# Where the first unit's products stand, and which engine scales the weight taps, in a convolution with batch norm and SiLU

## The chip, the cores and the metric

The kernel runs on one core of a Trainium2 chip. A core has five engines with queues of their own: TensorE (PE; its weight loads are listed as PEld), VectorE (DVE), ScalarE (ACT), GpSimd (POOL) and SyncE (SP), which here only issues transfers. The metric is the device time of one execution in microseconds (us); the time of a kernel is the median of its runs. Beside it there is one profiled execution, from which all lines of the profile are.

## The reference

A convolution of three taps along the sequence, with a 1024 x 1024 matrix for each tap, then batch norm with given statistics, then SiLU:

```python
B, S, C = 2, 2048, 1024
K = 3
xp = jnp.pad(x, ((0, 0), (P, P), (0, 0)))
y = sum(jnp.einsum('bsc,cd->bsd', xp[:, k:k + S, :], w[k]) for k in range(K))
inv_std = 1.0 / jnp.sqrt(var + 1e-5)
y = (y - mean) * (g * inv_std) + b
return _silu(y)
```

All inputs and the output are bf16.

## The kernel before

**The method.** Six neighbouring outputs are made at once from eight inputs (a Winograd convolution with six outputs and three taps). The sequence of 2048 falls into 342 such tiles. For each batch the eight combinations of the inputs (matrix `BT`) are made once, and for each the channel product with a combination of the three weight taps. So in place of 3 x 6 products of a tile there are 8, numbered 0 to 7. Products 0 and 7 use the raw taps w[0] and w[2]; products 1 to 6 use sums and differences of scaled taps. The outputs are then combinations of the eight products.

**Batch 0's windows** (L369 to L389 in the listing below: the first loop over `wi`). `x` arrives in 17 windows of 21 tiles (the last of 6) through SP's queue. For each window PE multiplies by the small matrix `Rm` (`transform`, L218; L230 in the profile), eight matmuls in two halves of four, each into a pair of PSUM banks, and ScalarE (L244) or VectorE (L246) casts the half to bf16 into `T_sb0`. Which of the two does it is decided while the kernel is built: `load` holds a planned time for each, and the smaller sum gets the cast. From window 10 on three pairs of banks are used in turn; banks 2 and 3 are then free for products. The raw taps of the first 128 output channels (chunk 0) come between windows 3, 8 and 16, tap w[1] last.

**Batch 1's windows.** The same for `T_sb1`, but in 51 groups of three, three and two matmuls, each into one of banks 4 to 7 in turn. Among them stand the products of the first unit.

**Units.** A unit is one chunk of 128 output channels for one batch: 8 products of 8 matmuls (one for each 128 input channels) with 342 moving columns. There are 8 x 2 units. `mms` (L248; L255 in the profile) is one product. `unit` (L274) yields after every matmul, and `run(gen, n)` takes the next n, which is how the first unit (unit 0) is spread among the transforms. The order of the products is 1, 3, 2, 4, 5, 7, 6, 0, in four banks A, B, C, G: 1 and then 2 into A, 3 and then 4 into B, 5 and then 6 into C, 7 into G. Between two products in one bank ScalarE copies the first one out (`copy_out`, L299; copies m1, m3, m5, s1, s2, L303 in the profile), and VectorE makes the outputs y0 to y5 from banks and copies (`stt`, L295; L296 and L340 in the profile). Product 2 cannot start before m1 is copied, 4 not before m3, 6 not before m5. Unit 0 alone has products 7 and 0 first: columns 0 to 188 (`seven_cut = 9 * WT`) of product 7 one or two matmuls at a time after windows 10 to 15, product 0 over all 342 columns after the last window, and its copy p0; the rest of product 7 stands before product 1 (half of it) and after product 5.

**The `late` list.** The SiLUs of a unit (`silu`, L265; L266 in the profile: y2 and y4 together, then y1, y3 and y5, then y0) are put on the list `late` and issued in the next unit, ahead of its copies; `pace` says how many ahead of which copy (m1, m3, s1, s2, m5 in order of issue); what is left goes after m5. `finish` issues the transposing transfer and the stores of an earlier unit on SP.

**Weight combinations.** For each chunk GpSimd makes three sums of w[0] and w[2] (`pair_sum`, L158: e1, e2, eh) and from each a sum and a difference with w[1] (`pair_tap`, L171), the weights `uch` of products 1 to 6. For this w[0] and w[2] are scaled by 4 and w[1] by 2 (`scale_weights`, L144): on ScalarE (L151), for chunk 0 on GpSimd (L149). From chunk 2 on VectorE makes e1 (`outer_by_reduce`, L165). Chunk 1's work is issued between unit 0 and unit 1 (chunk 0, batch 1): e1 and its two taps, then all three scalings, then the rest.

Every engine works through its own queue in the order in which the kernel text issues; nothing is reordered between engines but by semaphores.

Of the kernel before, what the change touches and what calls it, by code (L numbers as in the profile page):

```python
# [9 lines left out]
ALU = mybir.AluOpType  # L10
# [23 lines left out]
WT = 21  # L34
# [3 lines left out]
def kernel(  # L38
# [14 lines left out]
    CT = C // P  # L53
    DC = D // P
    assert S % P == 0 and C % P == 0 and D % P == 0
    NTB = (S + M_OUT - 1) // M_OUT
    assert NTB <= 512
    NWIN = (NTB + WT - 1) // WT
# [85 lines left out]
    def scale_weights(dc, taps=(2, 1, 0), on_gpsimd=False):  # L144
        for k in taps:
            f = 2.0 if k == 1 else 4.0
            dst = wx[dc, k] = wtmp.tile([P, CT, P], BF16, name=f"w{k}x")
            if on_gpsimd:
                nc.gpsimd.tensor_scalar(dst, raw[dc][k], f, 0.0, op0=ALU.mult, op1=ALU.add)  # L149
            else:  # L150
                nc.scalar.mul(dst, raw[dc][k], f)  # L151
# [24 lines left out]
    load = {"act": 0.0, "dve": 1.0}  # L176
# [68 lines left out]
        else:  # L245
            nc.vector.tensor_copy(dst, src)  # L246

    def mms(bk, j, dc, bi, c0, c1, start, at=0, cts=range(CT)):  # L248

        for ct in cts:  # L250
            if j in (0, 7):
                lhsT = raw[dc][0 if j == 0 else 2][:, ct, :]
            else:
                lhsT = wts[dc][:, j - 1, ct, :]
            nc.tensor.matmul(  # L255
                ps_all[:, bk * 512 + at:bk * 512 + at + c1 - c0],
                lhsT=lhsT,
                rhs=T_sb[bi][:, ct, j, c0:c1],
                start=start and ct == 0,
                stop=ct == CT - 1,  # L260
                skip_group_check=not start,
            )
            yield
# [7 lines left out]
            scale=sk[:, dc:dc + 1],  # L271
        )

    def unit(dc, bi, c0, c1, banks, yT, late, pace=(1, 0, 1, 1, 0), seven_cut=None, calls=None):  # L274

        nn = c1 - c0
        A, B_, C_, G = [ps_all[:, k * 512:k * 512 + nn] for k in banks]
        bA, bB, bC, bG = banks
        pace = list(pace)

        def et(name):
            return epool.tile([P, NTB], FP32, name=name)[:, 0:nn]

        m1, m3, m5, s1, s2, d1 = (et(n) for n in ("m1", "m3", "m5", "s1", "s2", "d1"))
        y_all = epool.tile([P, M_OUT, NTB], FP32, name="y")[:, :, 0:nn]
        y = [y_all[:, i if calls is None else ENDS.index(i)] for i in range(M_OUT)]

        def stt(o, i0, s, i1, op1=ALU.add):  # L295
            nc.vector.scalar_tensor_tensor(out=o, in0=i0, scalar=s, in1=i1, op0=ALU.mult, op1=op1)  # L296
            load["dve"] += 0.00123 * nn

        def copy_out(dst, src):  # L299
            for _ in range(pace.pop(0)):  # L300
                if late:
                    late.pop(0)()
            nc.scalar.copy(dst, src)  # L303
            load["act"] += 0.001 * nn

        if seven_cut:


            p0 = et("s2")
            yield from mms(bG, 7, dc, bi, c0, c0 + seven_cut, True)  # L310
            yield from mms(bC, 0, dc, bi, c0, c1, True)
            copy_out(p0, C_)
            yield from mms(bG, 7, dc, bi, c0 + seven_cut, c1, True, seven_cut, range(CT // 2))
        yield from mms(bA, 1, dc, bi, c0, c1, True)
        copy_out(m1, A)
        yield from mms(bB, 3, dc, bi, c0, c1, True)
        copy_out(m3, B_)
        yield from mms(bA, 2, dc, bi, c0, c1, False)
        copy_out(s1, A)
        stt(d1, m1, 2.0, A, op1=ALU.subtract)  # L320
        yield from mms(bB, 4, dc, bi, c0, c1, False)
        if seven_cut:
            for i in (2, 4, 0):
                stt(y[i], B_, ALPHA * (2.0 ** i), s1)
        else:
            copy_out(s2, B_)
            for i in (2, 4):
                stt(y[i], B_, ALPHA * 2.0 ** i, s1)
        stt(B_, m3, 2.0, B_, op1=ALU.subtract)
        yield from mms(bC, 5, dc, bi, c0, c1, True)  # L330
        copy_out(m5, C_)
        while late:
            late.pop(0)()
        for i in (1, 3, 5):
            stt(y[i], B_, ALPHA * 2.0 ** i, d1)
        if seven_cut:
            yield from mms(bG, 7, dc, bi, c0 + seven_cut, c1, True, seven_cut, range(CT // 2, CT))
        else:
            yield from mms(bG, 7, dc, bi, c0, c1, True)
        nc.vector.tensor_tensor(y[5], G, y[5], op=ALU.add)  # L340
        yield from mms(bC, 6, dc, bi, c0, c1, False)
        for i in (2, 4):
            stt(y[i], C_, BETA * 0.5 ** i, y[i])
        stt(G, m5, 2.0, C_, op1=ALU.subtract)
        if not seven_cut:
            yield from mms(bA, 0, dc, bi, c0, c1, False)
        for i in (1, 3, 5):
            stt(y[i], G, BETA * 0.5 ** i, y[i])
        if seven_cut:
            stt(y[0], C_, BETA, y[0])  # L350
            stt(y[0], p0, 1.0, y[0])
        else:
            stt(y[0], s2, ALPHA, A)
            stt(y[0], C_, BETA, y[0])

        if calls is None:
            late.extend(lambda i=i: silu(dc, yT, y_all, c0, c1, *i, 2) for i in ((2, 5), (1, 6), (0, 1)))
        else:
            late.extend(lambda i=i: silu(dc, yT, y_all, c0, c1, *i) for i in calls)
# [8 lines left out]
    units = [(dc, bi) for dc in range(DC) for bi in range(B)]  # L368
    late = []  # L369
    with tc.tile_pool(name="xwin", bufs=10) as xpool:  # L370
        first = unit(0, 0, 0, NTB, (0, 1, 2, 3), yTs[0], late, seven_cut=9 * WT)
        for wi in range(NWIN):
            window = load_window(xpool, 0, wi)
            if wi in (3, 8, NWIN - 1):
                load_chunk(0, {3: 2, 8: 0, NWIN - 1: 1}[wi])
            for h in range(2):
                bk = (2 * wi + h) % 4 * 2 if wi < 10 else (0, 6, 4)[(2 * wi + h - 20) % 3]
                transform(0, wi, window, 4 * h, 4, bk, 2, 2 if h == 0 and wi in (4, 9) else 0)
            if wi == 0:
                turn_params()  # L380
            if wi == 5:
                open_chunk(0)
                scale_weights(0, (2,), on_gpsimd=True)
            if wi == 8:
                pair_sum(0, 0)
                pair_sum(0, 1)
                scale_weights(0, (0,), on_gpsimd=True)

            run(first, {10: 1, 11: 1, 12: 1, 13: 1, 14: 2, 15: 2}.get(wi, 0))  # L389
        pair_tap(0, 0, ALU.add)  # L390
        scale_weights(0, (1,), on_gpsimd=True)
        for n, op in ((1, ALU.add), (0, ALU.subtract), (1, ALU.subtract)):
            pair_tap(0, n, op)
        pair_sum(0, 2)
        for op in (ALU.add, ALU.subtract):
            pair_tap(0, 2, op)
        make_params()
        load["act"] = load["dve"] = 0.0

        gi, done = 0, 8  # L400
        run(first, done)
        for wi in range(NWIN):
            window = load_window(xpool, 1, wi)
            for ct0, n in ((0, 3), (3, 3), (6, 2)):
                transform(1, wi, window, ct0, n, 4 + gi % 4, 3)
                gi += 1
                want = 8 + 44 * max(gi - 1, 0) // (3 * NWIN - 1)
                run(first, want - done)
                done = want
        for k in (0, 2, 1):  # L410
            load_chunk(1, k)
        load_weights(1)
        run(first)
# [41 lines left out]
    for ui, (dc, bi) in enumerate(units[1:-1], 1):  # L455
        yT = yTs[ui % 2]
        half = 4 * (ui % 2)
        if bi == 0 and dc + 1 < DC:
            outer_by_reduce(dc + 1)
        if bi == 1 and dc + 1 < DC:  # L460
            open_chunk(dc + 1)
            if dc == 0:
                pair_sum(1, 0)
                for op in (ALU.add, ALU.subtract):
                    pair_tap(1, 0, op)
                scale_weights(1)
            else:
                scale_weights(dc + 1)
            for n in range(0 if dc else 1, 3):
                if n:  # L470
                    pair_sum(dc + 1, n)
                for op in (ALU.add, ALU.subtract):
                    pair_tap(dc + 1, n, op)
        calls = ((0, 2), (2, 6)) if ui == len(units) - 2 else None
        run(unit(dc, bi, 0, NTB, (half, half + 1, half + 2, half + 3), yT, late, calls=calls))
        if ui < len(units) - 2:
            late.append(lambda dc=dc, bi=bi, yT=yT: finish(dc, bi, yT))
        if bi == 1 and dc % 2 == 1 and (dc + 3) // 2 < DC // 2:
            load_weights((dc + 3) // 2)
# [150 lines left out]
```

## Time and profile before

| | |
|---|---|
| time of the runs, median (lowest, highest) | 192.47 us (192.31, 192.87), 3 runs |
| the profiled execution: time / span | 192.21 us / 190.3 us |
| mean granted TensorE clock | 0.993 |
| PE, DVE, ACT, POOL busy, us | 179.7, 159.1, 124.9, 147.0 |
| first transform of batch 0 / of batch 1 | 4.16 / 22.11 us |
| last transform of batch 1 | 38.64 us |
| start of the long unbroken stretch of PE | 43.67 us |
| end of that stretch | 174.7 us |

The span runs from the first to the last instruction on the core; the time has 1.9 us more. The profile gives for each engine when it was busy, and for the chain that ended last which engine or transfer set the time at each moment. Matmuls are pipelined: the row of one ends some 0.17 us after the next could start, so prices of matmuls are taken from start to start, and "x8" in a row means eight instructions merged from the first start to the last end.

### The profile page before, as it was taken

What the parts mean: (1) busy time and instruction counts of PE and PEld (TensorE: products, weight loads), DVE (VectorE), ACT (ScalarE), POOL (GpSimd) and SP (SyncE); (2) the same over time, 40 slices, a digit from 0 to 9 for tenths busy, and PEclk for the clock granted to TensorE, in tenths of its full rate; (3) what the DMA queues carried; (4) which work ended last, traced back from release to release, by engine and by line L of the source; (5) the groups of instructions that cost most, each with busy time, mean ns of one, the idle gap of its engine ahead of it and who ended that gap; (6) DMA issues with size and microseconds to landing.
All of it is one profiled execution on the core that took longest, in us unless ns stands there. A gap on an engine that the chain in (4) does not pass through costs nothing.

```text
span 190.3 us, 3950 instructions
## 1 busy us (share of the span) xinstructions
PE 179.7 (94%) x1416; PEld 126.9 (67%) x1416; DVE 159.1 (84%) x343; ACT 124.9 (66%) x207; POOL 147.0 (77%) x88
## 2 busy tenths in 40 slices
PE   7897999999999999999999999999999999999960
PEld 3766788765666666666666666666666666669850
DVE  6577587997999699969996999699879988788981
ACT  3787798998378627763876487548745873625770
POOL 6537699999999996999699969996999699800000
PEclk9999999999999999999999999999999999999997
DMA  5999998940609298979293899874656556566425
GB/s 130 340 350 310 355 367 238 269 109 5 119 5 202 49 208 220 227 169 199 48 190 60 178 250 204 183 166 88 150 99 135 110 129 118 116 126 163 119 65 101
DMA packets 86759, 31.72 MB, mean 167 GB/s; under 512 B 73364, under 2 KB 82580, under 8 KB 86740
## 3 DMA queue, kind: packets, MB, share of 16 engines
q1 hardware_dynamic: 86637, 31.46, 70.2%
q8 instruction: 11, 0.18, 0.4%
q14 instruction: 8, 0.07, 0.1%
q10 hardware_dynamic: 103, 0.02, 0.0%
HBM read 14.82 MB, written 8.39 MB: 122 GB/s over the span
## 4 chain that ended last, share of the span: by engine, by line
PE 82%; ACT 5%; DMA 5%; DVE 3%; SPq 2%; issue 1%; DVEq 0%; ACTq 0%
PE ps_all L255 74%; PE ps_all L230 7%; DMA xw<-in_x_dram 5%; ACT yT L266 2%; ACT T_sb L244 1%; SPq L215 1%; DVE y L516 1%; PE ps_all L494 1%; DVE T_sb L246 1%; ACT w2x L151 1%; SPq L90 1%; ACT w1x L151 0%; DVE d L516 0%; ACT w0x L151 0%; DVE ps_all L516 0%
## 5 line engine op out<-in xcount | busy, mean ns | idle before, releaser
L255 PE MATMUL ps_all<-T_sb,uch 128*128 128x342 bf16 (+2 forms) x816 | 123.2, 299 | 0.6 <-ACT m L303 0.6
L255 PEld LDWEIGHTS <-uch 128*128 128x128 bf16 x816 | 77.0, 97 | 34.0 <-issue 1.0
L266 ACT ACTIVATE yT<-y,beta,sk 128x684 bf16<-128x684 f32 (+5 forms) x46 | 44.1, 960 | 29.2 <-DVE y L296 28.5
L255 PE MATMUL ps_all<-T_sb,wch 128*128 128x342 bf16 (+4 forms) x280 | 44.2, 296 | 0.3 <-DVE T_sb L246 0.3
L296 DVE SCALAR_TENSOR_TENSOR y<-ps_all,y 128x342 f32<-128x342 f32 x90 | 41.8, 508 | 1.3 <-PE ps_all L255 0.3
L173 POOL TENSOR_TENSOR uch<-e,wch 128x1024 bf16<-128x1024 f32 x16 | 33.8, 2133 | 10.7 <-DVE e L169 4.9
L173 POOL TENSOR_TENSOR uch<-e,w1x 128x1024 bf16<-128x1024 f32 x16 | 34.0, 2142 | 0.6
L173 POOL TENSOR_TENSOR uch<-eh,w1x 128x1024 bf16<-128x1024 f32 x16 | 33.8, 2134 | 0.6
L255 PEld LDWEIGHTS <-wch 128*128 128x128 bf16 x280 | 26.4, 97 | 11.4 <-issue 0.3
L303 ACT COPY m<-ps_all 128x342 f32<-128x342 f32 x45 | 19.8, 442 | 19.1 <-PE ps_all L255 18.6
L244 ACT CAST T_sb<-ps_all 128x672 bf16<-128x672 f32 (+5 forms) x50 | 27.7, 610 | 6.6 <-PE ps_all L230 5.8
L230 PE MATMUL ps_all<-Rm,xw 128*128 128x168 bf16 (+1 forms) x272 | 29.2, 238 | 1.5 <-ACT T_sb L244 0.6
L246 DVE CAST T_sb<-ps_all 128x504 bf16<-128x504 f32 (+4 forms) x35 | 23.2, 699 | 6.9 <-PE ps_all L230 6.4
L230 PEld LDWEIGHTS <-xw 128*128 128x128 bf16 (+1 forms) x272 | 22.5, 100 | 7.3 <-issue 3.3
L296 DVE SCALAR_TENSOR_TENSOR y<-ps_all,d 128x342 f32<-128x342 f32 x45 | 20.3, 507 | 0.5
L296 DVE SCALAR_TENSOR_TENSOR y<-ps_all,s 128x342 f32<-128x342 f32 x31 | 14.4, 507 | 3.3 <-ACT s L303 3.3
L163 POOL TENSOR_TENSOR e<-wch,w2x 128x1024 f32<-128x1024 bf16 x8 | 17.0, 2128 | 0.0
L163 POOL TENSOR_TENSOR eh<-w0x,wch 128x1024 f32<-128x1024 bf16 x8 | 17.0, 2127 | 0.0
L296 DVE SCALAR_TENSOR_TENSOR ps_all<-m,ps_all 128x342 f32<-128x342 f32 x30 | 15.3, 509 | 0.0
L296 DVE SCALAR_TENSOR_TENSOR d<-m,ps_all 128x342 f32<-128x342 f32 x15 | 7.6, 507 | 8.9 <-ACT s L303 8.9
L169 DVE TENSOR_REDUCE e<-wch 128x1024 f32<-128x2048 bf16 x6 | 13.7, 2276 | 0.0
L303 ACT COPY s<-ps_all 128x342 f32<-128x342 f32 x30 | 13.1, 438 | 0.1
(68 smaller groups left out, 85.3 us busy)
## 6 DMA issues: line engine op xcount, KB each, us to landing
xw<-in_x_dram SPq DMA_DIRECT2D x30, 256.0 KB
out_dram<-o_sb SPq DMA_DIRECT2D x30, 192.0 KB
wch<-in_w_dram SPq DMA_DIRECT2D x9, 512.0 KB
out_dram<-o_sb SPq DMA_DIRECT2D x15, 120.0 KB
wch<-in_w_dram SPq DMA_DIRECT2D x6, 256.0 KB
xw<-in_x_dram SPq DMA_DIRECT2D x2, 224.0 KB
out_dram<-o_sb SPq DMA_DIRECT2D x15, 7.5 KB
out_dram<-o_sb SPq DMA_DIRECT2D x15, 0.5 KB
```

The costliest lines, as they stand in the source:

```text
L90: nc.sync.dma_start(out=raw[dc][k], in_=w_all[:, k, :, dc * P:(dc + 1) * P])
L151: nc.scalar.mul(dst, raw[dc][k], f)
L163: engine.tensor_tensor(e, a, c, op=ALU.add)
L169: nc.vector.tensor_reduce(e, taps.rearrange("p k ct d -> p ct d k"), axis=mybir.AxisListType.X, op=ALU.add)
L173: nc.gpsimd.tensor_tensor(wts[dc][:, 2 * n + (op == ALU.subtract)], outer[dc, n], odd, op=op)
L230: nc.tensor.matmul(banks[:, at:at + NJ * ntile], lhsT=xw[0:kk, (ct0 + c) * P:(ct0 + c + 1) * P], rhs=Rm[0:kk, :, 0:ntile], start=True, sto ...
L244: nc.scalar.copy(dst, src)
L246: nc.vector.tensor_copy(dst, src)
L255: nc.tensor.matmul(ps_all[:, bk * 512 + at:bk * 512 + at + c1 - c0], lhsT=lhsT, rhs=T_sb[bi][:, ct, j, c0:c1], start=start and ct == 0, st ...
L266: nc.scalar.activation(yT[:, i0:i1:step, c0:c1], y_all[:, i0:i1:step], ACT.Silu, bias=beta[:, dc:dc + 1], scale=sk[:, dc:dc + 1],)
L296: nc.vector.scalar_tensor_tensor(out=o, in0=i0, scalar=s, in1=i1, op0=ALU.mult, op1=op1)
L303: nc.scalar.copy(dst, src)
```

## The change

Seven things are edited:

- `seven_cut` becomes `cut`, 11 windows (231 columns) instead of 9 (189). Product 7 and now also product 0 are made in two parts, columns 0 to 230 and 231 to 341.
- The first parts are issued after windows 13 (2 matmuls), 14 (2), 15 (4) and 16 (8), instead of one or two of product 7 after windows 10 to 15 and product 0 whole after the last window.
- The second part of product 0 (8 matmuls) stands behind the first three groups of batch 1's transforms; products 1, 3, 2, 4 and 5 and half of the second part of product 7 are spread over the other 48 groups. The second part of product 7 stands whole between products 5 and 6.
- Chunk 0: the scaling of w[1] goes from GpSimd to ScalarE; eh is made before the first tap instead of after the fourth.
- Chunk 1: of the three scalings only that of w[2] is issued ahead of unit 1, the other two from the `late` list, w[1] behind the copy m3 and w[0] behind the copy m5, with the sums and taps that need them.
- `pace` of unit 1 is (0, 1, 2, 1, 0) instead of (1, 0, 1, 1, 0).
- The planned cost of a copy on ScalarE is 0.0013 us for each column instead of 0.001.

```diff
@@ mms: the argument cts (a part of the channel tiles) goes @@
-    def mms(bk, j, dc, bi, c0, c1, start, at=0, cts=range(CT)):
-        for ct in cts:
+    def mms(bk, j, dc, bi, c0, c1, start, at=0):
+        for ct in range(CT):
@@ unit @@
-            load["act"] += 0.001 * nn
-        if seven_cut:
+            load["act"] += 0.0013 * nn
+        if cut:
             p0 = et("s2")
-            yield from mms(bG, 7, dc, bi, c0, c0 + seven_cut, True)
-            yield from mms(bC, 0, dc, bi, c0, c1, True)
+            yield from mms(bG, 7, dc, bi, c0, c0 + cut, True)
+            yield from mms(bC, 0, dc, bi, c0, c0 + cut, True)
+            yield from mms(bC, 0, dc, bi, c0 + cut, c1, True, cut)
             copy_out(p0, C_)
-            yield from mms(bG, 7, dc, bi, c0 + seven_cut, c1, True, seven_cut, range(CT // 2))
...
-        if seven_cut:
-            yield from mms(bG, 7, dc, bi, c0 + seven_cut, c1, True, seven_cut, range(CT // 2, CT))
+        if cut:
+            yield from mms(bG, 7, dc, bi, c0 + cut, c1, True, cut)
@@ batch 0's windows @@
-        first = unit(0, 0, 0, NTB, (0, 1, 2, 3), yTs[0], late, seven_cut=9 * WT)
+        first = unit(0, 0, 0, NTB, (0, 1, 2, 3), yTs[0], late, cut=11 * WT)
...
                 scale_weights(0, (0,), on_gpsimd=True)
-
-            run(first, {10: 1, 11: 1, 12: 1, 13: 1, 14: 2, 15: 2}.get(wi, 0))
+                pair_sum(0, 2)
+
+            run(first, {13: 2, 14: 2, 15: 4, 16: 8}.get(wi, 0))
         pair_tap(0, 0, ALU.add)
-        scale_weights(0, (1,), on_gpsimd=True)
-        for n, op in ((1, ALU.add), (0, ALU.subtract), (1, ALU.subtract)):
+        scale_weights(0, (1,))
+        for n, op in ((1, ALU.add), (0, ALU.subtract), (1, ALU.subtract), (2, ALU.add), (2, ALU.subtract)):
             pair_tap(0, n, op)
-        pair_sum(0, 2)
-        for op in (ALU.add, ALU.subtract):
-            pair_tap(0, 2, op)
         make_params()
         load["act"] = load["dve"] = 0.0
-
-        gi, done = 0, 8
-        run(first, done)
+        gi, done = 0, 0
@@ batch 1's windows @@
                 gi += 1
-                want = 8 + 44 * max(gi - 1, 0) // (3 * NWIN - 1)
+                want = 8 * gi // 3 if gi < 4 else 8 + 44 * (gi - 3) // (3 * NWIN - 3)
                 run(first, want - done)
@@ between unit 0 and unit 1 @@
-            if dc == 0:
-                pair_sum(1, 0)
-                for op in (ALU.add, ALU.subtract):
-                    pair_tap(1, 0, op)
-                scale_weights(1)
...
+                def sums(n, *taps):
+                    scale_weights(1, taps)
+                    pair_sum(1, n)
+                    for op in (ALU.add, ALU.subtract):
+                        pair_tap(1, n, op)
+
+                sums(0, 2)
+                late.insert(1, lambda: scale_weights(1, (1,)))
+                late.insert(2, lambda: sums(1))
+                late.append(lambda: sums(2, 0))
         calls = ((0, 2), (2, 6)) if ui == len(units) - 2 else None
-        run(unit(dc, bi, 0, NTB, (half, half + 1, half + 2, half + 3), yT, late, calls=calls))
+        run(unit(dc, bi, 0, NTB, (half, half + 1, half + 2, half + 3), yT, late, (1, 0, 1, 1, 0) if ui > 1 else (0, 1, 2, 1, 0), calls=calls))
```

For chunks 2 to 7 the scalings, sums and taps are issued in the same order as before.

More of the change, by code (lines that the diff above doesn't have):

```diff
@@ L272, in silu, with unit @@
         )
-    def unit(dc, bi, c0, c1, banks, yT, late, pace=(1, 0, 1, 1, 0), seven_cut=None, calls=None):
+    def unit(dc, bi, c0, c1, banks, yT, late, pace=(1, 0, 1, 1, 0), cut=None, calls=None):
         nn = c1 - c0
@@ L335, in unit @@
             stt(y[i], B_, ALPHA * 2.0 ** i, d1)
-        if seven_cut:
-            yield from mms(bG, 7, dc, bi, c0 + seven_cut, c1, True, seven_cut, range(CT // 2, CT))
+        if cut:
+            yield from mms(bG, 7, dc, bi, c0 + cut, c1, True, cut)
         else:
@@ L344, in unit @@
         stt(G, m5, 2.0, C_, op1=ALU.subtract)
-        if not seven_cut:
+        if not cut:
             yield from mms(bA, 0, dc, bi, c0, c1, False)
@@ L348, in unit @@
             stt(y[i], G, BETA * 0.5 ** i, y[i])
-        if seven_cut:
+        if cut:
             stt(y[0], C_, BETA, y[0])
@@ L461 @@
             open_chunk(dc + 1)
-            if dc == 0:
-                pair_sum(1, 0)
-                for op in (ALU.add, ALU.subtract):
-                    pair_tap(1, 0, op)
-                scale_weights(1)
-            else:
[L468 to L473, printed above, removed]
+            if dc:
+                scale_weights(dc + 1)
+                for n in range(3):
+                    if n:
+                        pair_sum(dc + 1, n)
+                    for op in (ALU.add, ALU.subtract):
+                        pair_tap(dc + 1, n, op)
+            else:
+                def sums(n, *taps):
+                    scale_weights(1, taps)
+                    pair_sum(1, n)
+                    for op in (ALU.add, ALU.subtract):
+                        pair_tap(1, n, op)
[3 more added lines that the diff above has]
+                late.append(lambda: sums(2, 0))
         calls = ((0, 2), (2, 6)) if ui == len(units) - 2 else None
-        run(unit(dc, bi, 0, NTB, (half, half + 1, half + 2, half + 3), yT, late, calls=calls))
+        run(unit(dc, bi, 0, NTB, (half, half + 1, half + 2, half + 3), yT, late, (1, 0, 1, 1, 0) if ui > 1 else (0, 1, 2, 1, 0), calls=calls))
         if ui < len(units) - 2:
```

## The prediction, made before the changed kernel had run

> **What bounds the kernel now.** I read the page first (busy shares, the chain that ended last), then the chain in order of time, then the timelines of PE and ScalarE around the two places where the chain leaves PE.
>
> ```profile
> PE 179.7 (94%) x1416; PEld 126.9 (67%) x1416; DVE 159.1 (84%) x343; ACT 124.9 (66%) x207; POOL 147.0 (77%) x88
> PE 82%; ACT 5%; DMA 5%; DVE 3%; SPq 2%; issue 1%; DVEq 0%; ACTq 0%
> ```
>
> PE is busy 94% of the 190.3 us span and carries 82% of the chain. Only where the chain is *not* on PE can a reordering win time. After the input transfers of the first 13.4 us these are the places that matter here:
>
> ```profile
> 20.54 0.37 DVE T_sb L246
> 20.91 0.04 issue
> 20.95 1.32 PE ps_all L255 x8
> ...
> 39.49 1.06 ACT w2x L151
> 40.55 0.94 ACT w1x L151
> 41.49 0.69 ACT w0x L151
> 42.18 0.16 issue
> 42.34 0.94 ACT yT L266
> 43.28 0.34 ACT m L303
> 43.62 0.04 issue
> 43.67 131.03 PE ps_all L255 x912
> ```
>
> Columns: start, length, what. From 43.67 on PE runs 131 us without a break, so everything earlier that delays 43.67 delays the end one for one, and nothing in those 131 us has to be gained. The PE timeline has a second wait just before:
>
> ```profile
> 38.95 0.43 PE L255 MATMUL ps_all<-T_sb,wch 128*128 128x153 bf16 x4
> ...
> 39.64 3.64 PE L255 MATMUL ps_all<-T_sb,uch 128*128 128x342 bf16 x24 [0.26 <-ACT m L303]
> ```
>
> A matmul row ends some 0.17 us after the next could start, so I count waits from start to start.
> (a) Window 16's last transform could be followed at 20.52; product 0 over all 342 columns starts at 20.95, after DVE's cast: 0.43.
> (b) Four matmuls of 0.07 from 38.95 end the queue at 39.23; product 6 starts at 39.64, after the copy m5: 0.41.
> (c) 24 matmuls of 0.145 from 39.64 reach 43.12; product 2 of unit 1 starts at 43.67, after the copy m1, which stood on ScalarE behind three scalings and a silu: 0.55.
> Together 1.39 us.
>
> **The change part by part.** *Products 7 and 0 cut at 231.* Before: 8 matmuls of 189 columns, 8 of 342, 8 of 153. After: 16 of 231 and 16 of 111. Prices from start to start: 189 columns 0.081 (15.28 to 15.36), 153 columns 0.066 (22.69 to 22.75), 342 columns 0.145 (170.20 to 171.36 for 8). The new widths have near neighbours, 229 and 113:
>
> ```profile
> 171.36 3.81 PE L255 MATMUL ps_all<-T_sb,uch 128*128 128x229 bf16 x37
> ...
> 179.13 2.55 PE L255 MATMUL ps_all<-T_sb,uch 128*128 128x113 bf16 x44
> ```
>
> 36 steps in 3.81 less one duration of 0.25 give 0.099; 43 steps in 2.55 less 0.21 give 0.054 (a short wait is in it). Before 8 x 0.081 + 8 x 0.145 + 8 x 0.066 = 2.34; after 16 x 0.099 + 16 x 0.054 = 2.45: **+0.11**. Bounds for 111 columns: 0.050 to 0.066 (the 153 row), so +0.05 to +0.30.
>
> *Where they stand.* The products after windows 13 and 14 fall into waits that stay (PE stops after 17.96 until 18.38 for a DVE cast). The four after window 15 cost 0.40 instead of 0.16, less 0.09 of wait: window 16 comes 0.15 later and ends at 20.67. Then 8 matmuls of product 0's first 231 columns, which need windows 0 to 10 alone, run to 21.46 while window 16 is cast. So (a) goes, and batch 1's transforms start at 21.46 instead of 22.11. SP's queue keeps its order; its wait for the first part of batch 1's window 0 ends at 21.07, so that data is there. The tails (8 of product 0 behind the first three groups, 4 of product 7 at the end of the loop) are in the +0.11.
>
> *Tap scaling w1x of chunk 0, POOL to ScalarE.* 1.04 on POOL (L149), 1.05 on ScalarE (L151; 0.95 start to start). It stands behind window 16's cast (ends 21.20) and ahead of all casts of batch 1. What hides it is this gap:
>
> ```profile
> 22.53 0.96 ACT L244 CAST T_sb<-ps_all 128x504 bf16<-128x504 f32 x2 [1.33 <-PE ps_all L230]
> ```
>
> Scaling 21.2 to 22.2; group 0's cast, which could start 0.42 after its matmuls (22.11 to 22.53 before), so at 21.88, starts at 22.15 and ends at 22.75. Its bank is wanted by group 4 at 21.46 + 11 x 0.0725 + 8 x 0.054 = 22.69: a wait of 0.1, as long as the one that PE had at the same place (22.97 + 0.07 to 23.19). **0**. Cover gone: up to 0.95.
> The Trainium skill (TensorE: Matmul & The Clock Gate, on engine queue depths) says that ScalarE's queue is a strict FIFO; by this rule a scaling whose tap has not landed would hold all casts behind it. The rows agree with the order (the copy m1 at 43.19 stands behind work that it does not need), and with a landing after 21.2 the sum would lose what it is late by. The landing that POOL waited for ended at 20.41, so I add nothing.
>
> *POOL.* eh (2.13) moves into POOL's idle 2.31 us before 20.41, and w1x leaves. The first tap still runs 20.41 to 22.54; product 1 first reads it at about 23.0. Later taps come up to 3.2 us sooner, and nothing waited for them: **0**. If the first tap were later than 23.0, PE would wait.
>
> *Copy m5.* Product 5 now ends some four groups before the loop does (44 matmuls over 48 groups instead of 50, no product 7 ahead of them), so its copy runs inside the loop: (b) goes. In the loop PE had three short waits near the copies m1, m3 and s1 (0.12, 0.12, 0.19 start to start); a fourth one of that size comes: **+0.14** (bounds 0 and 0.3).
>
> *Chunk 1's scalings apart.* Let T be the issue of batch 1's last transform. PE does 4 tails to T+0.2, product 6 to T+1.4, product 1 to T+2.5. ScalarE does w2x by T+1.3, the copy m1 at T+2.7 to 3.15; product 2 starts at T+3.7: (c) goes. Then silu, copy m3 to T+4.4 (product 4 wants it at T+4.8), w1x, copy s1, silu, copy s2 to T+7.2, copy m5 to T+7.8 (product 6 wants it at T+8.3), silu, w0x to T+9.3. POOL: eh to T+11.4, tap 13.6, tap 15.7; unit 2 starts at T+10.6 and reads them as products 5 and 6 at T+15.2 and T+17.5. Hidden, with at least 1.6 us. But s2 comes 3.4 us ahead of unit 2 instead of 4.0 (46.63 against 50.63), and DVE's outputs behind it 0.6 later against PE. In unit 2 the silu ended at 51.87, copy m1 at 52.49, product 2 at 52.95: 0.6 later just fits; unit 3 may wait a little: **+0.05** (0 to 0.3).
>
> **Sum.** -1.39 + 0.11 + 0.14 + 0.05 = **-1.09**. The profiled execution took 192.21 (span 190.33 and 1.88 around it), 0.26 under the median 192.47 of the three runs. 192.47 - 1.09 = **191.4**.
>
> **Rivals.**
> 1. *ScalarE becomes the loop's bound.*
>
> ```profile
> 22.50:38.90 16.40, 16.38 (x177) 13.43 (x175) 14.18 (x27) 15.21 (x34) 16.16 (x10) 1.00 1.02 299
> ```
>
> (PE, PEld, DVE, ACT, POOL busy.) ScalarE is busy 15.2 of 16.4 us here, and the planner of the casts does not count w1x. If its 0.95 comes back as PE waits: 191.4 + 0.95 = 192.3, no change. Against: the ring of four banks has DVE, with 2.2 us idle, on its other slots, and the gap of 1.33 takes the scaling.
> 2. *Slower: DVE late in unit 1.* The silu ahead of copy m3 needs y2 and y4 of unit 0; I have them at T+2.6. Up to T+3.1 nothing moves, up to T+3.6 PE does not notice; beyond, product 4 waits one for one, and the rest of ScalarE's chain with it. At 2.9 late: 191.4 + 1.9 = 193.3. For: three y operations now stand ahead of the last cast on DVE, and DVE is nearly full in the later units. Against: its 2.2 us idle in the loop.
> 3. *Better.* The short waits near copies vanish, as each group has a little more PE work than before: -1.39 + 0.11 - 0.43 = -1.71, 190.8.
> 4. *The change does not do what it says:* batch 1's first window or tap 1 lands late (the queue is at its full rate there), PE waits at 21.5 and (a)'s share is lost: 192.0.
>
> **How the numbers follow.** A measurement of this kernel can tell about 0.3% (0.58 us) from no change. Forecast 0.62 (own range 190.9 to 191.9), rival 1 0.17, rival 2 0.08, rival 3 0.08, rival 4 0.05. The range 190.7 to 192.3 takes the forecast, rival 4, half of rivals 1 and 3: 0.8. Faster (under 191.9): 0.62 + 0.08 = 0.70; same: rivals 1 and 4, 0.22; slower: 0.08.
>
> **What would show it.** Right: batch 1's first transform near 21.5; w1x on ScalarE between window 16's cast and group 0's; no PE wait at the end of the loop or ahead of unit 1's product 2; the unbroken PE stretch starting 1.1 us sooner. Wrong: PE waits for ScalarE's casts in the loop that sum to over 1 us (rival 1), a PE wait ahead of product 4 in unit 1 or product 2 in units 2 and 3 (rival 2), a PE wait for a transfer near 21.5 (rival 4), or product 1 waiting for POOL's first tap.

## The result: slower by 0.35%, and the profile after

The changed kernel takes 193.25 us (median of 20 runs, 192.74 to 193.90), against 192.59 (20 runs, 192.01 to 193.52) of the kernel before: ratio 1.0035, with an interval of 1.0024 to 1.0047. It was to be 1.09 us faster; it is 0.66 slower.

The page of the changed kernel, the parts with the busy times and with the shares of the chain:

```profile
PE 179.4 (94%) x1424; PEld 126.3 (66%) x1424; DVE 158.7 (83%) x343; ACT 125.7 (66%) x208; POOL 145.8 (76%) x87
...
PE 75%; DVE 9%; DMA 6%; ACT 4%; issue 2%; SPq 1%; DVEq 0%; ACTq 0%
```

Only ScalarE got more work: 125.7 us instead of 124.9, with the scaling w1x of chunk 0. But DVE holds 9% of the chain, where it held 3%, and PE 75% where it held 82%. So somewhere PE now waits for something that goes through VectorE. The chain in order of time (start, length, what) says where:

```profile
33.29 0.51 DVE d L296
33.80 0.61 DVE T_sb L246
...
34.45 0.30 PE ps_all L230 x2
...
39.88 7.34 PE ps_all L255 x53
...
47.29 0.45 ACT m L303
47.74 0.58 ACT yT L266
...
48.34 0.94 DVE y L296 x2
49.27 0.43 DVE ps_all L296
...
53.01 1.79 DVE y L296 x4
```

Two things are new. In the loop the chain leaves PE for `d1` (`d L296`) and a cast. And at 47.21 it leaves PE for the copy m5, a SiLU (`yT L266`) and then VectorE's first `y` of unit 1; there the kernel before had its unbroken stretch of PE. The PE timeline of the changed kernel shows what came of it (the end of a row: what PE waited for):

```profile
40.07 7.13 PE L255 MATMUL ps_all<-T_sb,uch 128*128 128x342 bf16 x48
...
50.52 2.49 PE L255 MATMUL ps_all<-T_sb,uch 128*128 128x342 bf16 x16
53.92 3.64 PE L255 MATMUL ps_all<-T_sb,uch 128*128 128x342 bf16 x24 [0.92 <-ACT m L303]
```

At the end of the loop and ahead of unit 1's product 2 (in the 48 matmuls from 40.07) PE no longer waits: the gains (b) and (c) are there. The new wait is one unit later, ahead of unit 2's product 2 (53.92).

To put numbers on it I take the starts of instructions as milestones. The start of the profiled executions differs for reasons that have nothing to do with the change (batch 0's window 9 begins at 13.43 in the one, 14.02 in the other, after the same transfers and the same work), so stages are counted from window 9 on:

| stage | before | after | difference | predicted |
|---|---|---|---|---|
| window 9 to batch 1's first transform, (a) | 8.68 | 8.15 | -0.53 | -0.65 |
| first to last transform (the loop) | 16.56 | 17.52 | +0.96 | +0.52 |
| to unit 1's product 1, (b) | 2.13 | 1.54 | -0.59 | -0.46 |
| to unit 1's product 2, (c) | 2.87 | 2.32 | -0.55 | -0.55 |
| to unit 2's product 1 | 6.96 | 6.97 | +0.01 | 0 |
| unit 2's product 1 to 2 | 2.32 | 3.40 | +1.08 | +0.05 for this row and the next but one |
| to unit 3's product 1 | 6.97 | 6.96 | -0.01 | 0 |
| unit 3's product 1 to 2 | 2.32 | 2.55 | +0.23 | |
| to the end of the span | 128.09 | 128.08 | -0.01 | 0 |
| sum | 176.90 | 177.49 | **+0.59** | **-1.09** |

In the last column the forecast's +0.11 for the matmuls is spread over the rows in which they stand: -0.22 in (a), +0.38 in the loop, -0.05 in (b).

The sum of +0.59 is close to the 0.66 between the medians, so these stages hold nearly the whole result. Of the 1.68 us between forecast and measurement, 1.26 are in units 2 and 3 and 0.44 in the loop; (a) and (b) differ by 0.12 and 0.13 in opposite directions.

**Units 2 and 3.** VectorE of the changed kernel around unit 1, then ScalarE (start, length, instruction, and in brackets the idle time before it with its releaser):

```profile
48.34 0.94 DVE L296 SCALAR_TENSOR_TENSOR y<-ps_all,s 128x342 f32<-128x342 f32 x2 [2.22 <-ACT yT L266]
```

```profile
46.60 0.44 ACT L303 COPY s<-ps_all 128x342 f32<-128x342 f32 x1
47.29 0.45 ACT L303 COPY m<-ps_all 128x342 f32<-128x342 f32 x1 [0.25 <-PE ps_all L255]
47.63 0.67 ACT L266 ACTIVATE yT<-y,beta,sk 128x342 bf16<-128x342 f32 x1
...
52.58 0.96 ACT L266 ACTIVATE yT<-y,beta,sk 128x684 bf16<-128x684 f32 x1 [3.33 <-DVE y L296]
53.45 0.77 ACT L303 COPY m<-ps_all 128x342 f32<-128x342 f32 x2
```

Unit 1's y2 and y4 (`y<-ps_all,s`) need the copy s2, which ends at 47.04. They start at 48.34, and the releaser is no copy but the SiLU `yT` of 47.63. That SiLU does not make anything they read: it is unit 0's last one, of y0. It *reads* unit 0's `y`. The tile `y` has one buffer, and a new unit opens a new tile in it; the first write to the new tile waits for all reads of the old one, also of slices that this write doesn't touch. Unit 1's new pace (0, 1, 2, 1, 0) leaves this SiLU over until after the copy m5, and m5 waits for product 5 (the 0.25 `<-PE`). From 48.34 on VectorE has one piece of work after the other until unit 1's y2 and y4 are final (52.54); on them wait unit 2's SiLU (3.33 idle) and, behind that in ScalarE's queue, the copy m1, and on this PE.

In the kernel before, the last SiLU stood ahead of s2, the same y operations were released by s2, and unit 2's products 1, 3, 2, 4 and 5 were one row (ScalarE, VectorE and PE of that kernel):

```profile
45.42 0.67 ACT L266 ACTIVATE yT<-y,beta,sk 128x342 bf16<-128x342 f32 x1
46.18 0.45 ACT L303 COPY s<-ps_all 128x342 f32<-128x342 f32 x1
...
46.66 0.94 DVE L296 SCALAR_TENSOR_TENSOR y<-ps_all,s 128x342 f32<-128x342 f32 x2 [0.59 <-ACT s L303]
...
50.63 5.97 PE L255 MATMUL ps_all<-T_sb,uch 128*128 128x342 bf16 x40
```

**The loop.** VectorE and then PE of the changed kernel:

```profile
33.29 0.51 DVE L296 SCALAR_TENSOR_TENSOR d<-m,ps_all 128x342 f32<-128x342 f32 x1 [0.74 <-ACT s L303]
33.72 1.26 DVE L246 CAST T_sb<-ps_all 128x504 bf16<-128x504 f32 x2
```

```profile
33.49 0.31 PE L255 MATMUL ps_all<-T_sb,uch 128*128 128x342 bf16 x1
34.45 0.30 PE L230 MATMUL ps_all<-Rm,xw 128*128 128x168 bf16 x2 [0.65 <-DVE T_sb L246]
```

`d1` needs the copy s1. It stands at the head of VectorE's queue for 0.74 us until s1 comes, and behind it stands a cast, which needs nothing of the kind and whose bank PE wants. PE waits 0.82 from start to start (33.49 + 0.145 to 34.45). The copy s1 is late itself: product 2 ends at 32.06, and s1 starts at 32.81, behind a cast on ScalarE. In the kernel before VectorE had a cast of its own to do ahead of `d1`, and no idle time between the two:

```profile
33.19 0.68 DVE L246 CAST T_sb<-ps_all 128x504 bf16<-128x504 f32 x1 [0.37 <-PE ps_all L230]
33.80 0.51 DVE L296 SCALAR_TENSOR_TENSOR d<-m,ps_all 128x342 f32<-128x342 f32 x1
```

### The profile page after: what moved, and what is told of

Read it like the earlier page. It is cut to its first block, busy times and chain, and to the rows that moved or that the text cites. A ratio compares the mean times of both kernels' runs of the same rounds, so it can differ in the third digit from the quotient of the medians.

```text
span 191.5 us, 3966 instructions
## 1 busy us (share of the span) xinstructions
PE 179.4 (94%) x1424; PEld 126.3 (66%) x1424; DVE 158.7 (83%) x343; ACT 125.7 (66%) x208; POOL 145.8 (76%) x87
## 4 chain that ended last, share of the span: by engine, by line
PE 75%; DVE 9%; DMA 6%; ACT 4%; issue 2%; SPq 1%; DVEq 0%; ACTq 0%
PE ps_all L255 68%; PE ps_all L230 7%; DMA xw<-in_x_dram 6%; DVE y L296 4%; ACT yT L266 2%; ACT T_sb L244 1%; DVE y L519 1%; PE ps_all L497 1%; DVE T_sb L246 1%; DVE ps_all L296 1%; DVE y L340 1%; DVE d L296 1%; ACT m L303 0%; SPq L215 0%; DVE e L169 0%
## 5 line engine op out<-in xcount | busy, mean ns | idle before, releaser
L266 ACT ACTIVATE yT<-y,beta,sk 128x684 bf16<-128x684 f32 (+5 forms) x46 | 44.1, 960 | 30.3 <-DVE y L296 29.6
L296 DVE SCALAR_TENSOR_TENSOR y<-ps_all,y 128x342 f32<-128x342 f32 x90 | 41.9, 508 | 1.6 <-PE ps_all L255 0.6
L244 ACT CAST T_sb<-ps_all 128x672 bf16<-128x672 f32 (+4 forms) x50 | 27.8, 612 | 6.5 <-PE ps_all L230 5.5
L230 PEld LDWEIGHTS <-xw 128*128 128x128 bf16 (+1 forms) x272 | 21.5, 98 | 9.3 <-issue 3.4
L296 DVE SCALAR_TENSOR_TENSOR y<-ps_all,d 128x342 f32<-128x342 f32 x45 | 20.3, 507 | 0.5
L296 DVE SCALAR_TENSOR_TENSOR y<-ps_all,s 128x342 f32<-128x342 f32 x31 | 14.4, 508 | 5.0 <-ACT s L303 2.8
L296 DVE SCALAR_TENSOR_TENSOR ps_all<-m,ps_all 128x342 f32<-128x342 f32 x30 | 15.3, 509 | 0.0
L296 DVE SCALAR_TENSOR_TENSOR d<-m,ps_all 128x342 f32<-128x342 f32 x15 | 7.6, 507 | 9.1 <-ACT s L303 9.1
```

The lines of the kernel that those rows point to most:

```text
L230: nc.tensor.matmul(banks[:, at:at + NJ * ntile], lhsT=xw[0:kk, (ct0 + c) * P:(ct0 + c + 1) * P], rhs=Rm[0:kk, :, 0:ntile], start=True, sto ...
L266: nc.scalar.activation(yT[:, i0:i1:step, c0:c1], y_all[:, i0:i1:step], ACT.Silu, bias=beta[:, dc:dc + 1], scale=sk[:, dc:dc + 1],)
```

## The experiments

Two theories: *turn-over* (the wait in units 2 and 3 comes from the first write to the new `y`, held by unit 0's last SiLU) and *d1* (the loop's loss is `d1` waiting ahead of casts). Against them stand the prediction's first rival (ScalarE has too much work in the loop, by the scaling w1x), its second (y2 and y4 of unit 0 late for the SiLU ahead of m3), and the simpler account that in units 2 and 3 VectorE is late because copies and scalings on ScalarE came later. All ratios are against the kernel before (192.59 us for the changed one, 192.60 in experiments 1 to 4, 192.50 in 5 to 8).

| kernel | median, us | ratio [95%] | loop | wait ahead of unit 2's / 3's product 2 | window 9 to end |
|---|---|---|---|---|---|
| before | | | 16.56 | 0 / 0 | 176.90 |
| changed | 193.25 | 1.0035 [1.0024, 1.0047] | 17.52 | 1.08 / 0.23 | 177.49 |
| 1 one tile y for units 0 and 1 | 192.01 | 0.9956 [0.9938, 0.9974] | 17.53 | 0 / 0.04 | 176.24 |
| 2 last SiLU ahead of s2 | 192.53 | 0.9992 [0.9973, 1.0012] | 17.52 | 0.44 / 0.22 | 176.85 |
| 3 d1 later | 192.43 | 0.9992 [0.9973, 1.0011] | 16.72 | 1.08 / 0.23 | 176.70 |
| 4 w1x back on GpSimd | 193.39 | 1.0037 [1.0023, 1.0052] | 17.58 | 1.08 / 0.22 | 177.61 |
| 5 repairs 1 and 3 | 191.10 | 0.9913 [0.9885, 0.9941] | 16.72 | 0 / 0.05 | 175.44 |
| 6 as 5, old cost of copies | 191.47 | 0.9933 [0.9907, 0.9959] | 16.86 | 0 / 0.05 | 175.57 |
| 7 before + chunk 1's part alone | 193.21 | 1.0034 [1.0014, 1.0054] | 16.56 | 1.08 / 0.23 | 177.65 |
| 8 changed without chunk 1's part | 192.63 | 1.0010 [0.9988, 1.0033] | 17.53 | 0 / 0 | 177.09 |

### 1. Units 0 and 1 share one tile y

```diff
-        y_all = epool.tile([P, M_OUT, NTB], FP32, name="y")[:, :, 0:nn]
+        if (dc, bi) != (0, 1):
+            y_kept[0] = epool.tile([P, M_OUT, NTB], FP32, name="y")
+        y_all = y_kept[0][:, :, 0:nn]
```

Where no new tile is opened, each write waits only for the reads of its own slice.

> The changed kernel, but unit 1 writes its outputs y into the same tile as unit 0 instead of opening a new one in the same buffer; no engine's order changes. Theory (turn-over of y): VectorE's first y operation of unit 1 no longer waits for the last SiLU of unit 0 (which the new pace puts behind copy m5); it starts right behind copy s2, about 1.3 us sooner, PE's waits ahead of product 2 in unit 2 (1.08 us) and unit 3 (0.23 us) shrink to 0.1 us together or less, and the ratio to the kernel before falls from 1.0035 to about 0.997. Rival (VectorE is late from unit 0's own y operations, or from the scaling ahead of copy s1): the first y operation starts at most 0.2 us sooner, both waits stay, ratio about 1.0035.

VectorE, then PE of this kernel:

```profile
46.47 0.94 DVE L298 SCALAR_TENSOR_TENSOR y<-ps_all,s 128x342 f32<-128x342 f32 x2 [0.96 <-ACT s L305]
```

```profile
49.90 5.97 PE L255 MATMUL ps_all<-T_sb,uch 128*128 128x342 bf16 x40
```

The releaser is now the copy s2 (45.99 to 46.44), and unit 2's products 1, 3, 2, 4 and 5 are one row of 40 matmuls without a wait. ScalarE's work and its order are the same as in the changed kernel, the last SiLU still behind m5. So copies and scalings coming later on ScalarE can't be the cause: the turn-over alone cost the 1.24 us between the medians (1.25 in the stages).

### 2. The last SiLU ahead of the copy s2, with a new tile

```diff
-                sums(0, 2)
-                late.insert(1, lambda: scale_weights(1, (1,)))
-                late.insert(2, lambda: sums(1))
+                sums(0, 2, 1)
+                sums(1)
                 late.append(lambda: sums(2, 0))
-        ... (1, 0, 1, 1, 0) if ui > 1 else (0, 1, 2, 1, 0) ...
+        ... (1, 0, 1, 1, 0) if ui > 1 else (0, 1, 1, 1, 0) ...
```

The scaling of w[1] goes back ahead of unit 1, and the SiLU of y0 moves ahead of s2, so that m5 holds nothing.

> The changed kernel, but chunk 1's scaling of w[1] stands ahead of copy m1 (beside that of w[2]) and the three SiLUs of unit 0 all stand ahead of copy s2, as in the kernel before; only the scaling of w[0] stays late. Theory (turn-over of y): as the last SiLU is then done before copy s2, the waits in units 2 and 3 go to 0.1 us or less, unit 1's product 2 still does not wait (ScalarE has 1.3 us idle ahead of copy m1), ratio about 0.997. Rival (VectorE late from unit 0's y operations): the wait ahead of product 2 of unit 2 stays near 1 us, ratio about 1.0035.

Only a part of it came: 0.44 us of the 1.08 stay, and 0.22 in unit 3. VectorE, ScalarE and GpSimd of this kernel:

```profile
44.92 1.98 DVE L296 SCALAR_TENSOR_TENSOR y<-s,y 128x342 f32<-128x342 f32 x1
...
47.98 0.94 DVE L296 SCALAR_TENSOR_TENSOR y<-ps_all,s 128x342 f32<-128x342 f32 x2 [0.65 <-ACT s L303]
```

```profile
46.95 0.67 ACT L266 ACTIVATE yT<-y,beta,sk 128x342 bf16<-128x342 f32 x1 [0.87 <-DVE y L296]
47.52 0.42 ACT L303 COPY s<-ps_all 128x342 f32<-128x342 f32 x1
```

```profile
44.41 4.50 POOL L173 TENSOR_TENSOR uch<-e,w1x 128x1024 bf16<-128x1024 f32 x2
```

VectorE's releaser is the copy s2 again, as meant. But s2 is itself late: it stands behind the SiLU of y0, and that waits 0.87 us for unit 0's last y0 operation, which took 1.98 us here and 0.52 in the changed kernel. The repair ran into another cost, with GpSimd at work beside it (last section).

Four kernels together show how late VectorE may be. Unit 1's first y operation starts so long ahead of unit 2's product 1: before 3.97 us (wait 0), experiment 1 3.43 (0), experiment 2 2.83 (0.44), changed 2.18 (1.08). From 2.83 to 2.18 the wait grows by 0.64 for 0.65; extended back, it begins near 3.3 (an estimate from these two points). The prediction had s2 come 3.4 us ahead of unit 2, and it did (47.04 against 50.52, 3.48): by that alone nothing would have been lost.

### 3. d1 later on VectorE

```diff
-        stt(d1, m1, 2.0, A, op1=ALU.subtract)
+        if cut:
+            load["dve"] += 0.00123 * nn
+        else:
+            stt(d1, m1, 2.0, A, op1=ALU.subtract)
         yield from mms(bB, 4, dc, bi, c0, c1, False)
         if cut:
+            load["dve"] -= 0.00123 * nn
+            stt(d1, m1, 2.0, A, op1=ALU.subtract)
```

In unit 0 d1 is issued after product 4. Its planned load is counted at the old place, so that the planner gives each cast to the same engine as in the changed kernel.

> The changed kernel, but in unit 0 alone VectorE's d1 is issued after product 4 instead of right behind copy s1, so that three casts stand ahead of it; the split of the casts between the engines is the same. Theory (d1 waits in order for copy s1 on ScalarE and holds a cast whose bank PE needs): PE's wait of 0.8 us near 34.4 us goes to 0.2 us or less, the stretch from batch 1's first to its last transform falls from 17.5 us to 16.8 us, ratio about 1.000. Rival (the casts as a whole fill both engines in this stretch, the scaling among them): the wait moves to another group, the stretch stays within 0.2 us of 17.5, ratio about 1.0035.

VectorE of this kernel in the same stretch:

```profile
30.69 2.92 DVE L246 CAST T_sb<-ps_all 128x336 bf16<-128x336 f32 x5
34.00 1.34 DVE L246 CAST T_sb<-ps_all 128x504 bf16<-128x504 f32 x2 [0.39 <-PE ps_all L230]
35.26 0.50 DVE L296 SCALAR_TENSOR_TENSOR d<-m,ps_all 128x342 f32<-128x342 f32 x1
```

VectorE now runs its casts and waits for PE, not PE for it. The loop takes 16.72 instead of 17.52: 0.80 us for moving one operation of 0.51 us, as long as PE's wait of 0.82 had been. The copy s1 starts no sooner (18.80 us after window 9, 18.79 in the changed kernel): its lateness cost PE time only through d1. Units 2 and 3 kept their waits to 0.01 us: the two causes are independent.

### 4. The scaling w1x of chunk 0 back on GpSimd

```diff
-        scale_weights(0, (1,))
+        scale_weights(0, (1,), on_gpsimd=True)
```

> The changed kernel, but chunk 0's scaling of w[1] is back on GpSimd, behind the first tap. Theory (the scaling on ScalarE is hidden in the gap before batch 1's first cast): the stretch from batch 1's first to its last transform stays within 0.2 us of 17.5, ratio 1.0035 within 0.001. Rival 1 of the prediction (the scaling comes back as waits for ScalarE's casts): the stretch shortens by 0.5 to 0.95 us, ratio about 0.9995.

The loop is no shorter (17.58 against 17.52), so ScalarE's added work is not what fills it. ScalarE of the changed kernel shows the cover that the prediction named:

```profile
21.68 1.06 ACT L151 ACTIVATE w1x<-wch 128x1024 bf16<-128x1024 bf16 x1
22.64 1.73 ACT L244 CAST T_sb<-ps_all 128x504 bf16<-128x504 f32 x3
```

The scaling starts when window 16's casts are done, and the first cast of batch 1 follows at 22.64, 0.5 us after its matmuls began.

### 5 and 6. Both repairs; and the old planned cost of a copy

Experiment 5 has the edits of 1 and 3. Experiment 6 has, besides, `load["act"] += 0.001 * nn` as before.

> The changed kernel with both repairs: unit 1 writes y into unit 0's tile, and d1 of unit 0 is issued after product 4. Theory: the two losses are independent, so they add: 193.25 less 1.25 less 0.8 gives 191.2, ratio to the kernel before about 0.9915, no wait of PE above 0.15 us ahead of product 2 in units 2 and 3 nor near 34 us. Rival: they overlap (with the loop shorter, VectorE is later against PE in unit 1 and PE waits in unit 2 again), ratio 0.995 or more.

> As the kernel with both repairs, but the planned cost of a copy on ScalarE is 0.001 us per column again, as in the kernel before, so that some casts go to the other engine. Theory: the cost decides only small waits in the loop (0.3 us in all near 37 us); the time stays within 0.25 us, ratio 0.9915 within 0.0015. Rival: the new cost is what the loop's stretch hangs on; the stretch from batch 1's first to its last transform changes by 0.5 us or more.

Experiment 5 is 0.87% faster than before, the best version, and its chain has no break from unit 0's product 6 on:

```profile
39.54 134.76 PE ps_all L255 x941
```

Counted from window 9 it is 1.46 us shorter than before; the two repairs gained 2.05 together (1.25 and 0.79 alone). With the old planned cost the loop is 0.14 longer; the medians 191.10 and 191.47 lie 0.37 apart, more than the 0.25 expected, but from 6 runs each, and the intervals of their ratios overlap. That the new cost helps here is seen in one profile and not established by the times.

### 7 and 8. The change taken apart

Experiment 7 is the kernel before with chunk 1's scalings apart and the new pace, and nothing else. Experiment 8 is the changed kernel without these two.

> The kernel before with one part of the change alone: chunk 1's scalings taken apart and the pace of unit 1. Theory (turn-over of y): the wait of 0.55 us ahead of product 2 of unit 1 goes, and waits of about 1.1 us ahead of product 2 of unit 2 and 0.2 us in unit 3 come, as VectorE's first y operation of unit 1 now waits for the last SiLU; together 0.75 us more, ratio about 1.004. Rival (the waits in units 2 and 3 come from the earlier start of unit 1 that the cut gives, not from this part): only the gain stays, ratio about 0.997.

> The changed kernel without the part for chunk 1 (its scalings stand together again, pace as before): the cut at 231, the new places, the scaling of chunk 0 on ScalarE and the planned cost remain. Theory: batch 1 starts 0.5 us sooner, the loop is 0.95 us longer (most of it the wait at d1), product 6 does not wait (0.6 us sooner), but product 2 of unit 1 then waits some 0.95 us instead of 0.55 for copy m1 behind three scalings; units 2 and 3 do not wait; together about +0.25 us, ratio 1.001. Rival (the long wait in the loop comes from the part for chunk 1): the loop is as before, ratio 0.996.

PE of experiment 7, then of experiment 8:

```profile
53.79 2.48 PE L255 MATMUL ps_all<-T_sb,uch 128*128 128x342 bf16 x16 [0.92 <-ACT m L303]
```

```profile
44.08 2.19 PE L255 MATMUL ps_all<-T_sb,uch 128*128 128x342 bf16 x14 [0.73 <-ACT m L303]
```

Experiment 7 gains the 0.55 of (c) and loses 1.08 + 0.23, the same as in the changed kernel: chunk 1's part costs by itself, whatever is done in the loop. Its y operation had the same releaser and the same 2.22 us idle before it as the changed kernel's. Experiment 8 has nothing of this, but the wait of 0.55 ahead of unit 1's product 2 has become 0.90 (3.22 between products 1 and 2, against 2.32 without a wait): the loop ends with less for PE to do, product 2 is wanted sooner, and the copy m1 still stands behind three scalings. What (a) and (b) gained goes into this wait and into d1's.

## Why the prediction was wrong

- **(a), (b), (c): right.** The three waits are gone: -0.53, -0.59, -0.55. For (a), batch 1 starts 8.15 us after window 9 (22.17).
- **Products 7 and 0 cut at 231, and w1x: right.** The narrow matmuls need no more than they were given, and experiment 4 shows w1x hidden. GpSimd gained one wait (1.8 us for chunk 1's w1x) that nobody waits for.
- **"Copy m5", the fourth short wait of +0.14: mis-sized.** From start to start, all waits of PE in the loop sum to 0.96 before and 1.50 after: +0.54 in place of +0.14. The wait at s1 grew from 0.19 to 0.82, and three of 0.12, 0.06 and 0.15 came at 37.5 to 38.3; against them the waits near m1 and m3 shrank from 0.12 each to 0.05 and nothing, and two at the start of the loop (0.15 and 0.08) are gone. The step asked which copies would now fall into the loop, not what stands on VectorE behind an operation that waits for one. The kernel before had a wait of 0.19 near s1, and the step left it at that size. Experiment 3 gives 0.80 back. The prediction has no term for the new planned cost of a copy. Adding up `load` by the listing (the casts of each engine come out as in the traces) shows that it moved casts: with the new places, VectorE's first cast behind d1 is that of group 31 with the new cost and of group 33 with the old (counted from 0), whose bank PE wants later. So the new cost may have had a part in the wait. How large a part stays open: experiment 8 has both edits and the same loop, and no run has d1 at its place with the old cost.
- **"Chunk 1's scalings apart", +0.05: the step that failed.** "s2 comes 3.4 us ahead of unit 2" and "DVE's outputs behind it 0.6 later against PE": right for s2 (3.48) and wrong for the outputs, which started 1.79 later (3.97 us ahead of unit 2 before, 2.18 after). The step let VectorE start when its inputs were there. It followed the SiLU of y0 to its new place behind m5 (it stands in the list of that step), asked what it delays on ScalarE, and did not ask who waits for it. That is unit 1's first write to `y`. In place of 0.05 came 1.31; experiment 1 takes away all but 0.04 of it.
- **Rival 1 (ScalarE the bound of the loop): refuted** by experiment 4. The loop lost time, but for d1.
- **Rival 2 (slower, VectorE late): the kind of outcome, another mechanism.** PE does wait for a copy behind a SiLU that waits for y2 and y4. But they are unit 1's, not unit 0's, the product is 2 of unit 2 and not 4 of unit 1, and the lateness comes from the buffer of `y`. A wait ahead of product 2 in units 2 and 3 is among the signs that the prediction gave for this rival; the sign came, by a path that the rival did not describe. Unit 0's y2 and y4 were in time: no wait in 48 matmuls from 40.07.
- **Rivals 3 and 4:** of the three short waits near copies one vanished and one shrank, but s1's grew to 0.82; and no transfer was late at 22.

So the idea was sound and worth 1.46 us (experiment 5, from window 9) with its two side effects removed, more than the 1.09 forecast. Part of the surplus is not the idea's: d1's new place also ended the wait of 0.19 near s1, which the kernel before had already, and no run moved d1 in that kernel alone.

## What to carry to other kernels

When an operation is moved back, ask two things of it: what it now delays on its own engine, and who waits for it. The second list is longer than its data: where a tile has one buffer, the first write to the next tile waits for every reader of the old, and the last reader sets the start of the next stage. And in an in-order queue an operation that waits for a late input is as expensive as everything behind it, above all where a cast that frees a PSUM bank stands there; issue it later, when its input is there.

## What the runs showed that I had not expected

One operation of VectorE has very different lengths. It is unit 0's last y0 operation, `y<-s,y`, of which both inputs are in SBUF. In the changed kernel, then in the kernel before:

```profile
44.63 0.52 DVE L296 SCALAR_TENSOR_TENSOR y<-s,y 128x342 f32<-128x342 f32 x1
```

```profile
44.21 0.96 DVE L296 SCALAR_TENSOR_TENSOR y<-s,y 128x342 f32<-128x342 f32 x1
```

In experiment 2 it took 1.98. With 0.52, GpSimd was idle (43.6 to 45.4). With 0.96, GpSimd had a sum running from 42.67 to 44.79, and the operation ended 0.38 after that. With 1.98, GpSimd had started its first tap 0.5 us before (44.41 to 46.54), the operation ended 0.37 after that, and the two taps took 4.50 together where they took 4.21 beside no such operation. All ten profiles go one of these two ways: in five GpSimd was idle and the operation took 0.51 or 0.52; in the other five a GpSimd operation was running when it started, and it ended 0.37 or 0.38 after that one, whatever its length (0.66 to 1.98). The Trainium skill (SBUF — State Buffer, "Who interferes with whom") says that a VectorE instruction with two inputs in SBUF contends with a GpSimd instruction that reads SBUF, as its second input comes through a read interface that both share, and that issue order decides who blocks. The ten lengths agree with that; no run here changed this alone, so for this kernel it is a reading and not shown.

The start of an execution moves by itself: over the ten profiles window 9's first matmul, behind the same transfers, came between 13.40 and 14.49 us. That is more than the whole effect of this change, and a reason to compare profiles stage by stage.
